# A two-layer attention and MLP kernel: spreading the reciprocal denominators by quarters of the TensorE array, residual loads one by one, and a different split of the first loads

## The chip, the core and the metric

The kernel runs on one core of a Trainium2 chip. The core has TensorE (PE, matmuls into PSUM, whose weight loads are listed as PEld), VectorE (DVE), ScalarE (ACT), GpSimd (POOL) and SyncE (SP, which here only issues DMAs); they run side by side and meet through semaphores. SBUF is the on-chip memory of 128 partitions, PSUM holds matmul results in eight banks of 128 x 512 f32. The metric is the device time of one execution in microseconds. Before the change the median of 3 runs is 766.76 us (766.41 to 767.0).

## What is computed

Four layers, A, B, A, B, on x of 2048 tokens x 576, the same weights each time. Both kinds normalise first (B twice) and add their result to x.

```python
def _A_ref(x, wqkv, wo):                      # linear attention, H = 32 heads of 18
    q, k, v = (x @ wqkv) split by three and by heads
    phi = lambda t: jnp.where(t > 0, t + 1, jnp.exp(t)) + 1e-6
    pq, pk = phi(q), phi(k)
    kv = jnp.einsum("bhsd,bhse->bhde", pk, v)
    z = jnp.einsum("bhsd->bhd", pk)
    num = jnp.einsum("bhqd,bhde->bhqe", pq, kv)
    den = jnp.einsum("bhqd,bhd->bhq", pq, z)[..., None] + 1e-6
    return merge_heads(num / den) @ wo
def _B_ref(x, w1, b1, w2, b2):                # MLP, F = 4608
    h = _gelu(_layernorm(x) @ w1 + b1)
    return h @ w2 + b2
x = x + _A_ref(_layernorm(x), ...); x = x + _B_ref(_layernorm(x), ...)   # and both once more
```

The division by `den` belongs to one head and one token. The kernel applies it to `pq`: each row of `pq` (a feature of a head) is multiplied by 1/den of its head.

## The kernel before

All weights lie in SBUF. The tokens are 16 tiles of 128 (`NT`) and 4 blocks of 512 (`c`, `NCA`), four tiles `j` to a block. The 576 features of q, k and v are in 5 groups of 7, 7, 7, 7 and 4 heads (`G`; 126 rows, the last 72). In this text the layers are counted 1 to 4; in the code `li` runs from 0, so the attention layers are `li == 0` (layer 1) and `li == 2` (layer 3, where `li > 0`).

The order of TensorE's instructions is the order in the source (`pe`, L138). The order on the other engines is made by a scheduler from the dependences, its own estimate of times and the order in the source; `tc.add_manual_dep(..., NOSYNC)` fixes that one instruction comes behind another on its engine without a semaphore. A tile from a pool waits until a buffer of its tag is free. PSUM is used as four single banks (`ps_h`, tag "h") and two pairs (`accA`, `accB`).

**The start.** `load_x0(t)` (L145) loads a token tile of x, `load_wqkv(part)` (L150) a third of the qkv weights in two DMAs (part 1 the keys, 2 the values). `chained` puts all of them on SP's queue in source order (L156 to L166). ACT's table for exp and ln is asked for at L176. Then, tile by tile, layer 1 normalises (`LNPipe`), transposes on TensorE, projects keys, values and part of the queries, and sums kv.

**The second half of an attention layer** (from L747). `kv_wo(g)` folds kv of a group with `wo`. Then, for a token block c:
- `den_stage(c)` (L750): 20 matmuls on 32-column quarters of the array sum the denominators; quarter j of the partitions has the 32 heads of token tile j. ACT takes ln and exp(-x), which gives `rden` [128 x 128] in bf16. `rden` has one buffer.
- `quad_stage(c)` (L769): DVE spreads `rden` to a [128 x 512] tile in which each token tile's columns have their own 32 rows and zeros elsewhere (`quad_mask`).
- `scale_stage(g, c)` (L779): one matmul of 512 columns by `head_bc` repeats each head's value over its 18 rows; ACT copies the product from PSUM to SBUF as bf16 (L788), and DVE multiplies `pq` by it (L789). With `direct` DVE reads PSUM and ACT does nothing.
- `wo_stage(t)` (L793): the output tile, ten matmuls into accA or accB in turn, then `residual` (L504): DVE adds x, SP stores the sum to `x_d`. For the first four tiles the normalisation of the next MLP layer is fed (L803) with a `hold` (ticks to wait), a `tp_at` (the output tile from which its transpose may run on TensorE) and the engine of its statistics: ACT for even tiles (two passes, L333 and L342, behind the inverted denominators), DVE for odd ones.

Block 0 goes first (L811 to L833), with the last deferred queries and the denominators of block 1. Then the loop over t (L834): in iteration t it prefetches the residual rows of tile t+4, runs `wo_stage(t)`, makes `quad_stage` of a block whose denominators have come, projects one group of queries if any is left (three in layer 1, one in layer 3), spreads groups 0 to 2 of the next block at j = 0 and groups 3 and 4 at j = 1, and at j = 1 sums the denominators of the block after that. At t = 13 ACT loads the table of gelu. One or two ticks of `LNPipe` follow.

**Residual rows.** In layer 1 they are loaded in pairs of tiles from x in bf16, in layer 3 one by one from `x_d` in f32 (`prefetch_xo`, L486) into a pool of 9 row buffers (tag "row"), which the sums also use. `turned` (L110) is the SBUF tile in which the MLP layers turn their normalised rows; in the attention loops it is idle.

The MLP layers (`LayerB`) run 36 groups of first-product matmuls on two halves of the array's rows, with gelu on ACT, and 16 tiles of second-product matmuls.

Of the kernel before, what the change touches and what calls it, by code (L numbers as in the profile page):

```python
# [8 lines left out]
ALU = mybir.AluOpType  # L9
# [6 lines left out]
P = 128  # L16
# [18 lines left out]
def build(tc, A_x, A_wqkv, A_wo, B_w1, B_b1, B_w2, B_b2, out, dbg=None, n_layers=4):  # L35
    nc = tc.nc
    dbg = dbg or {}
    with ExitStack() as ctx:
# [103 lines left out]
                pe_chain["last"] = inst.ins.name  # L142
            return inst

        def load_x0(t):  # L145
            x0 = blk.tile([P, D], BF16, name="x0", tag="blk")
            chained(nc.sync.dma_start(out=x0[:], in_=x_in[t * P:(t + 1) * P, :]))
            x0_tiles[t] = x0

        def load_wqkv(part):  # L150
# [2 lines left out]
                                      in_=A_wqkv[0:4 * P, cols].rearrange("(k p) n -> p k n", p=P)))  # L153
            chained(nc.sync.dma_start(out=wqkv_sb[0:64, 4, cols], in_=A_wqkv[4 * P:D, cols]))

        load_x0(0)  # L156
        load_x0(1)
        load_wqkv(1)
        load_x0(2)
        load_wqkv(2)  # L160
        load_x0(3)
        load_x0(4)
# [10 lines left out]
                pe(nc.tensor.matmul(warm_ps[:], lhsT=y_ring[NY - 1][:, 0:P], rhs=y_ring[NY - 1][:, 0:512],  # L173
                                    start=True, stop=True))

        nc.scalar.preload_act_table_set("natural_log_exp_and_others")  # L176
        nc.vector.memset(wqkv_sb[64:P, 4, :], 0.0)
        for vr in v_ring:
            nc.gpsimd.memset(vr[:, 4, 72:126], 0.0)
# [306 lines left out]
        def prefetch_xo(li, t, add_b2):  # L486
            if li == 0:
                if t % 2 == 0:
                    pair = rows.tile([P, 2, D], BF16, name="xo_pair", tag="row")
                    chained(nc.sync.dma_start(  # L490
                        out=pair[:], in_=x_in[t * P:(t + 2) * P, :].rearrange("(two p) d -> p two d", two=2)))
                    for i in range(2):
                        xo_of[(li, t + i)] = pair[:, i, :]
                return
            xo = row_tile("xo")
            load = nc.sync.dma_start(out=xo[:], in_=x_d[t])
            if not add_b2:
                behind(load, "landed")
            if add_b2:
                tc.add_manual_dep(load.ins, dve_last["sum"], NOSYNC, reason="no residual rows ahead of their stage")  # L500
                nc.gpsimd.tensor_tensor(out=xo[:], in0=xo[:], in1=b2_bc[:], op=ALU.add)  # L501
            xo_of[(li, t)] = xo[:]

        def residual(li, t, halves):  # L504
            xo = xo_of.pop((li, t))
            last = (li == n_layers - 1)
            if last:
                xn = rows.tile([P, 2 * D], BF16, name="xbf", tag="row")[:, 0:D]
            elif li == 0:
                xn = row_tile("xn")[:]  # L510
            else:
                xn = xo
            parts = [slice(h * HALF, (h + 1) * HALF) for h in range(2)] if last and t == NT - 1 else [slice(0, D)]
            for i, cols in enumerate(parts):
                if len(parts) == 2:
                    total = nc.vector.tensor_tensor(out=xn[:, cols], in0=halves[i][:, 0:HALF], in1=xo[:, cols], op=ALU.add)
                else:
                    total = nc.vector.tensor_tensor(out=xn[:, cols].rearrange("p (h n) -> p h n", h=2), in0=halves,  # L518
                                                    in1=xo[:, cols].rearrange("p (h n) -> p h n", h=2), op=ALU.add)
                dve_last["sum"] = total.ins.name  # L520
                if last:
                    nc.sync.dma_start(out=out_f[t * P:(t + 1) * P, cols], in_=xn[:, cols])
            if last:
                return None
            nc.sync.dma_start(out=x_d[t], in_=xn)
            return xn

        def layer_A(li, next_kind, pre_a1=None):
# [217 lines left out]

            quad_rden = {}  # L747
            rden_of = {}

            def den_stage(c, after=None, pair=None):  # L750
                if pair:
# [11 lines left out]
                if after is not None:  # L763
                    tc.add_manual_dep(log.ins, after, NOSYNC, reason="copies first")
                act_last["rden"] = nc.scalar.activation(out=rden[:], in_=dp[:, P:2 * P], func=ACT.Exp,
                                                        scale=-1.0).ins.name
                rden_of[c] = rden

            def quad_stage(c, after=None):  # L769
                quad = blk.tile([P, D], BF16, name="quad_rden", tag="blk")  # L770
# [8 lines left out]
            def scale_stage(g, c, pair=None, direct=False):  # L779
# [10 lines left out]
                                               in1=spread_rows[0:GR[g], 0:CA], op=ALU.mult)  # L790
                dve_last["mult"] = mult.ins.name

            def wo_stage(t):  # L793
                c, j = divmod(t, TPC)
                wp = ps_acc.tile([P, 2, 512], F32, name="wo_ps", tag=("accA", "accB")[t % 2])
# [4 lines left out]
                                              start=(g == 0), stop=(g == G - 1)))  # L800
                xn = residual(li, t, wp[:, :, 0:HALF])
                if xn is not None and next_kind == "B" and t < TPC:
                    lnp.feed(xn, t, "B", "pool", "act", hold=(2, 2, 6, 6)[t], tp_at=6 + 2 * t,  # L803
                             **(dict(after="sum") if t % 2 else dict(stats="act", after="rden")))

            for t in range(AHEAD):
                prefetch_xo(li, t, add_b2=False)
            if "b1" in bias_stage:
                bias_casts()
# [12 lines left out]
            if li == 0:  # L822
                late = [q_proj(*q_left.pop(0), defer=True)]
            for g in range(3):
                scale_stage(g, 0)
            kv_wo(4)
            scale_stage(3, 0, pair="accA")
            late.append(q_proj(*q_left.pop(0), defer=True))
# [4 lines left out]
                phi(after=act_last["rden"])  # L833
            for t in range(NT):  # L834
                c, j = divmod(t, TPC)
                if t + AHEAD < NT:
                    prefetch_xo(li, t + AHEAD, add_b2=False)
                wo_stage(t)
                for late in list(rden_of):
                    quad_stage(late, after=dve_last["sum"])  # L840
                if q_left:
                    q_proj(*q_left.pop(0))
                if c + 1 < NCA:
                    for g in ((0, 1, 2), (3, 4), (), ())[j]:
                        scale_stage(g, c + 1)
                if j == 1 and c + 2 < NCA:
                    den_stage(c + 2)
                if t == NT - 3:
                    warm_table(ACT.Gelu_apprx_tanh, act_last["copy"])
                state["wo"] = t  # L850
# [240 lines left out]
```

## Time and profile before

| | |
|---|---|
| median of 3 runs | 766.76 us |
| profiled execution, device time | 766.11 us |
| its span, first to last instruction | 764.4 us |
| key and query work of layer 1, up to its last kv sum | to about 69 us |
| layer 1: from there to the MLP's first matmul | 69 to 106 us |
| layer 2 (MLP) | 106 to 388 us |
| layer 3 (attention) | 388 to 479 us |
| layer 4 (MLP) | 479 to 764 us |

The profile shows one execution. The page has the busy time of each engine, the busy shares in 40 slices, the TensorE clock that was granted, the DMA queues, and the chain that ended last: followed back from the last instruction, at each step to what released it or to the instruction before it on its engine. In rows of the chain of waits the columns are start, length (both us from the span's start) and what ran. In rows of the timeline they are start, length, engine, line, operation, output<-input, shapes and count, with the idle time before it and what ended that in brackets. In rows of groups they are line, engine, operation, names, shapes, count, then busy us, mean ns of one, and idle time in front with its releasers. TensorE's records overlap: a matmul of 512 columns has a record of about 0.38 us, but the next one starts 0.22 us later.

### The profile page before, as it was taken

To read this page: it belongs to the slowest core of one execution; us is meant where nothing else is said; L and a number is where in the kernel's file an instruction comes from. 1 tells how busy PE (TensorE), PEld (TensorE's weight loads), DVE (VectorE), ACT (ScalarE), POOL (GpSimd) and SP (SyncE) were. 2 spreads that over 40 slices of the span, in tenths; PEclk is the share of its full clock that TensorE was granted. 3 is DMA by queue.
4 is the path that set the end of the run, shared out by engine and by line. 5 is a ranking of instruction groups with operands and counts; after the bars stand their busy time and mean duration, and the time that the engine had idled before them with its cause. 6 is when DMAs were issued, how large, how long until landed. Compare 5 with 4: busy or idle time off the path is not lost.

```text
span 764.4 us, 15650 instructions
## 1 busy us (share of the span) xinstructions
PE 758.8 (99%) x6522; PEld 492.1 (64%) x6522; DVE 271.6 (36%) x684; ACT 336.5 (44%) x751; POOL 123.4 (16%) x198
## 2 busy tenths in 40 slices
PE   8999999999999999999999999999999999999998
PEld 6776664675477457646777767447745764674476
DVE  7785963135113603400355678600240032000000
ACT  5888856304710650164056577570064036205600
POOL 4681222012000301200110004200020021001000
PEclk9999999999999999999999999999999999999999
DMA  9992473016401721330246007530231033011000
GB/s 262 270 299 49 158 275 85 17 47 178 110 24 63 203 62 42 97 85 1 75 120 215 1 16 245 206 81 17 62 105 41 16 125 81 9 32 55 2 9 24
DMA packets 80289, 73.82 MB, mean 97 GB/s; under 512 B 36698, under 2 KB 64858, under 8 KB 80218
## 3 DMA queue, kind: packets, MB, share of 16 engines
q1 hardware_dynamic: 80218, 72.82, 32.6%
q8 instruction: 51, 0.84, 0.5%
q14 instruction: 20, 0.16, 0.1%
HBM read 48.03 MB, written 24.77 MB: 95 GB/s over the span
## 4 chain that ended last, share of the span: by engine, by line
PE 98%; DVE 1%; DMA 1%; ACT 0%; SPq 0%; issue 0%
PE m_ps L972 36%; PE h_ps L914 20%; PE hp_ps L914 16%; PE q_ps L588 5%; PE wo_ps L798 5%; PE k_ps L540 3%; PE k_ps L612 3%; PE k_ps L629 2%; PE v_ps L561 1%; PE m_half L972 1%; PE v_ps L558 1%; PE rden_ps L784 1%; PE tp L423 1%; DMA wqkv_sb<-in_A_wqkv_dram 1%; PE kvacc L582 1%; PE k_tail L629 1%
## 5 line engine op out<-in xcount | busy, mean ns | idle before, releaser
L972 PE MATMUL m_ps<-w_sb,hT 128*128 128x288 bf16 x2232 | 274.8, 286 | 0.0
L972 PEld LDWEIGHTS <-hT 128*128 128x128 bf16 x2304 | 224.8, 98 | 59.8 <-issue 3.4
L914 PEld LDWEIGHTS <-w_sb 64*128 64x128 bf16 x2304 | 124.5, 94 | 136.5 <-issue 1.9
L914 PE MATMUL hp_ps<-yT,w_sb 64*128 64x512 bf16 x1152 | 178.0, 376 | 0.0
L914 PE MATMUL h_ps<-yT,w_sb 64*128 64x512 bf16 x1152 | 148.0, 376 | 0.0
L919 ACT COPY relay_sb<-relay_sb 128x1 f32<-128x1 f32 x144 | 28.6, 198 | 262.3 <-PE h_ps L914 220.0
L910 ACT ACTIVATE hT<-h_ps,b1T 128x512 bf16<-128x512 f32 x144 | 91.2, 684 | 44.4 <-PE h_ps L914 44.4
L374 POOL TENSOR_TENSOR ln_rstd<-ln_u,neg_half 128x1 f32<-128x1 f32 x64 | 36.6, 574 | 370.8 <-DVE ln_u L365 226.4
L910 ACT ACTIVATE hT<-hp_ps,b1T 128x512 bf16<-128x512 f32 x144 | 91.2, 693 | 0.0
L518 DVE TENSOR_TENSOR xbf<-m_ps,xo 128x576 bf16<-128x576 f32 x15 | 11.4, 757 | 212.9 <-PE m_ps L972 212.9
L518 DVE TENSOR_TENSOR xo<-m_ps,xo 128x576 f32<-128x576 f32 x16 | 12.1, 758 | 176.1 <-PE m_ps L972 176.1
L501 POOL TENSOR_TENSOR xo<-xo,b_bc 128x576 f32<-128x576 f32 x32 | 41.0, 1287 | 100.4 <-DMA xo<-x_d 63.7
L914 PE MATMUL h_ps<-yT,w_tail 64*128 64x512 bf16 x144 | 54.1, 376 | 0.0
L914 PE MATMUL hp_ps<-yT,w_tail 64*128 64x512 bf16 x144 | 54.1, 376 | 0.0
L588 PE MATMUL q_ps<-yT,wqkv_sb 128*126 128x512 bf16 (+1 forms) x200 | 49.8, 380 | 0.0
L798 PE MATMUL wo_ps<-kvwo,pq 126*128 126x288 bf16 (+1 forms) x320 | 43.3, 286 | 0.5 <-DVE pq L789 0.5
L914 PEld LDWEIGHTS <-w_tail 64*128 64x128 bf16 x288 | 27.1, 94 | 17.1
L798 PEld LDWEIGHTS <-pq 126*128 126x128 bf16 (+1 forms) x320 | 30.1, 97 | 10.5 <-DVE pq L789 1.0
L467 ACT ACTIVATE phi_e<-k_ps 128x288 bf16<-128x288 f32 x46 | 19.3, 419 | 38.8 <-PE k_ps L612 35.8
L588 PEld LDWEIGHTS <-wqkv_sb 128*126 128x126 bf16 (+1 forms) x200 | 24.9, 131 | 11.4 <-issue 0.2
L475 DVE TENSOR_SCALAR phi_e<-phi_e 128x288 bf16<-128x288 bf16 (+2 forms) x86 | 24.7, 288 | 20.1 <-ACT phi_e L467 19.4
L467 ACT ACTIVATE phi_e<-q_ps 126x512 bf16<-126x512 f32 (+1 forms) x40 | 23.8, 596 | 18.0 <-PE q_ps L588 18.0
(136 smaller groups left out, 657.0 us busy)
## 6 DMA issues: line engine op xcount, KB each, us to landing
xo<-x_d SPq DMA_DIRECT2D x48, 288.0 KB
x_d<-xo SPq DMA_DIRECT2D x32, 288.0 KB
xl<-x_d SPq DMA_DIRECT2D x24, 288.0 KB
y_d<-turned SPq DMA_DIRECT2D x40, 144.0 KB
w_sb<-in_B_w_dram SPq DMA_DIRECT2D x6, 864.0 KB
yT<-y_d SPq DMA_DIRECT2D x10, 512.0 KB
w_sb<-in_B_w_dram SPq DMA_DIRECT2D x9, 512.0 KB
x_d<-xn SPq DMA_DIRECT2D x16, 288.0 KB
```

What stands on the lines that cost most here:

```text
L374: nc.gpsimd.tensor_tensor(out=rstd[:], in0=it["u"][:], in1=neg_half[:], op=ALU.pow)
L467: exp = nc.scalar.activation(out=e_out, in_=ps_ap, func=ACT.Exp)
L475: low = nc.vector.tensor_scalar(out=e[0:rows, 0:n], in0=e[0:rows, 0:n], scalar1=1.0, scalar2=1e-6, op0=ALU.min, op1=ALU.add)
L501: nc.gpsimd.tensor_tensor(out=xo[:], in0=xo[:], in1=b2_bc[:], op=ALU.add)
L518: total = nc.vector.tensor_tensor(out=xn[:, cols].rearrange("p (h n) -> p h n", h=2), in0=halves, in1=xo[:, cols].rearrange("p (h n) -> p ...
L588: pe(nc.tensor.matmul(qp[0:GR[g], :], lhsT=wqkv_sb[:, k, GO[g]:GO[g] + GR[g]], rhs=yT[:, k, c * CA:(c + 1) * CA], start=(k == 0), stop=(k ...
L629: pe(nc.tensor.matmul(dst, lhsT=lhsT, rhs=pk, start=(t == 0), stop=(t == NT - 1)))
L798: pe(nc.tensor.matmul(wp[:, half, 0:HALF], lhsT=pq[(g, c)][0:GR[g], j * P:(j + 1) * P], rhs=kvwo[g][0:GR[g], half * HALF:(half + 1) * HALF ...
L910: act_last["gelu"] = nc.scalar.activation(out=to, in_=ps, func=ACT.Gelu_apprx_tanh, bias=b1T[:, f:f + 1], scale=1.0).ins.name
L914: mm = pe(nc.tensor.matmul(dst[n], lhsT=wt, rhs=mv, start=(seen[n] == 0), stop=(seen[n] == 8)))
L919: relay = nc.scalar.copy(out=relay_sb[:, 1:2], in_=relay_sb[:, 0:1])
L972: pe(nc.tensor.matmul(acc[half][:, 0:HALF], lhsT=hT[f][:, j * P:(j + 1) * P], rhs=w2_sb[:, f, half * HALF:(half + 1) * HALF], start=(f == ...
```

## The change

The four full groups of token blocks 1 to 3 are spread in a new way in both attention layers. `quarter_stage(c)` takes `rden` as it is: for each group and each token tile i one matmul of 32 rows (i's heads) and 128 columns, each i into a PSUM bank of its own, 16 matmuls in all. ACT then copies the four banks to `turned`. `quarter_scale(c, groups)` multiplies `pq` of these groups by it, behind the output tile's sum. Group 4 goes as before, so `quad_stage` stays. The steps move in the loop: for block 1 the quarter stage stands behind output tile 1, its multiplies, group 4 and the denominators of block 2 behind tile 2; the later blocks' quarter stages stand behind tiles 3 and 7, their multiplies behind the two tiles after those, the denominators of block 3 behind tile 5. The queries left stand behind tile 0 (one) and tile 2 (two).

In layer 1 group 0 of block 0 is multiplied out of PSUM. In layer 3 six residual tiles are prefetched in place of four ahead of the loop, then one in each iteration from 1 to 10, and the loads of tiles 9 and up stand behind the last store. The statistics of the fed tiles change engines (DVE for even tiles, ACT for odd ones), with other holds, and in layer 1 other transposes. At the start ACT's table is asked for first, and token tiles 1 and 2 are loaded from ACT's queue behind it.

```diff
-        def load_x0(t):
+        def load_x0(t, by_act=False):
             x0 = blk.tile([P, D], BF16, name="x0", tag="blk")
-            chained(nc.sync.dma_start(out=x0[:], in_=x_in[t * P:(t + 1) * P, :]))
+            if by_act:
+                load = nc.scalar.dma_start(out=x0[:], in_=x_in[t * P:(t + 1) * P, :])
+                tc.add_manual_dep(load.ins, table.ins.name, NOSYNC, reason="table first")
+            else:
+                chained(nc.sync.dma_start(out=x0[:], in_=x_in[t * P:(t + 1) * P, :]))
...
+        table = nc.scalar.preload_act_table_set("natural_log_exp_and_others")
         load_x0(0)
-        load_x0(1)
+        load_x0(1, by_act=True)
         load_wqkv(1)
-        load_x0(2)
+        load_x0(2, by_act=True)
         load_wqkv(2)
...
-        nc.scalar.preload_act_table_set("natural_log_exp_and_others")
...
                 behind(load, "landed")
+                if t >= 9:
+                    tc.add_manual_dep(load.ins, sp_last["store"], NOSYNC, reason="stores first")
...
-            nc.sync.dma_start(out=x_d[t], in_=xn)
+            sp_last["store"] = nc.sync.dma_start(out=x_d[t], in_=xn).ins.name
...
+                rden_now["tile"] = rden
...
+            def quarter_stage(c):
+
+                rden = rden_now["tile"]
+                banks = [ps_h.tile([P, 512], F32, name="rden_ps", tag="h") for _ in range(4)]
+                for g in range(4):
+                    for i in range(4):
+                        rows = slice(32 * i, 32 * (i + 1))
+                        pe(nc.tensor.matmul(banks[i][0:126, g * P:(g + 1) * P], lhsT=head_bc[rows, g, 0:126],
+                                            rhs=rden[rows, :], start=True, stop=True))
+                spread_rows = turned[:].rearrange("p a t c -> p (a t c)").rearrange("p (i w) -> p i w", i=4)
+                for i in range(4):
+                    act_last["copy"] = nc.scalar.copy(out=spread_rows[0:126, i, 0:4 * P], in_=banks[i][0:126, :]).ins.name
+
+            def quarter_scale(c, groups, after):
+                spread_rows = turned[:].rearrange("p a t c -> p (a t c)").rearrange("p (i w) -> p i w", i=4)
+                for g in groups:
+                    scaled = pq[(g, c)][0:126, 0:CA].rearrange("p (i n) -> p i n", i=4)
+                    mult = nc.vector.tensor_tensor(out=scaled, in0=scaled,
+                                                   in1=spread_rows[0:126, :, g * P:(g + 1) * P], op=ALU.mult)
+                    tc.add_manual_dep(mult.ins, after, NOSYNC, reason="sums first")
+                    dve_last["mult"] = mult.ins.name
...
-                    lnp.feed(xn, t, "B", "pool", "act", hold=(2, 2, 6, 6)[t], tp_at=6 + 2 * t,
-                             **(dict(after="sum") if t % 2 else dict(stats="act", after="rden")))
-
-            for t in range(AHEAD):
+                    lnp.feed(xn, t, "B", "pool", "act", hold=(2, 2, 2, 4)[t] if li > 0 else (2, 8, 8, 10)[t], tp_at=6 + 2 * t if li > 0 else (6, 10, 11, 14)[t],
+                             **(dict(after="sum") if t % 2 == 0 else dict(stats="act", after="rden")))
+
+            for t in range(AHEAD if li == 0 else AHEAD + 2):
                 prefetch_xo(li, t, add_b2=False)
...
             for g in range(3):
-                scale_stage(g, 0)
+                scale_stage(g, 0, direct=(li == 0 and g == 0))
...
-                if t + AHEAD < NT:
-                    prefetch_xo(li, t + AHEAD, add_b2=False)
+                if li == 0 and t + AHEAD < NT or 0 < t < NT - AHEAD - 1 and li > 0:
+                    prefetch_xo(li, t + AHEAD + (li > 0), add_b2=False)
                 wo_stage(t)
-                for late in list(rden_of):
-                    quad_stage(late, after=dve_last["sum"])
-                if q_left:
+                total = dve_last["sum"]
+                if c + 1 < NCA:
+                    for g in ((), (), (0, 1, 2, 3), ())[j] if c == 0 else ((0, 1), (2, 3), (), ())[j]:
+                        quarter_scale(c + 1, (g,), after=total)
+                    if t == 1:
+                        quarter_stage(1)
+                    if j == 3 and c + 2 < NCA:
+                        quarter_stage(c + 2)
+                    if j == (2 if c == 0 else 0):
+                        scale_stage(4, c + 1)
+                if j == (2 if c == 0 else 1) and c + 2 < NCA:
+                    den_stage(c + 2)
+                    if c > 0:
+                        quad_stage(c + 2, after=total)
+                if t == 3:
+                    quad_stage(2, after=total)
+                if q_left and t in (0, 2):
                     q_proj(*q_left.pop(0))
-                if c + 1 < NCA:
-                    for g in ((0, 1, 2), (3, 4), (), ())[j]:
-                        scale_stage(g, c + 1)
-                if j == 1 and c + 2 < NCA:
-                    den_stage(c + 2)
+                    if t == 2:
+                        q_proj(*q_left.pop(0))
```

1 line of the change is left out of this document (added).

## Prediction

> **What bounds the kernel now.** I read the page's busy shares first, then its chain, then the chain in order of time around the two places that change.
>
> ```profile
> span 764.4 us, 15650 instructions
> PE 758.8 (99%) x6522; PEld 492.1 (64%) x6522; DVE 271.6 (36%) x684; ACT 336.5 (44%) x751; POOL 123.4 (16%) x198
> PEclk9999999999999999999999999999999999999999
> PE 98%; DVE 1%; DMA 1%; ACT 0%; SPq 0%; issue 0%
> ```
>
> TensorE is busy 99% of the span at the full granted clock, and 98% of the chain that ended last is its own. So time is gained only by fewer TensorE columns, or in the few places where TensorE stands. The changed loop of layer 1, and the place just in front of it, in the chain of waits (start, length, what):
>
> ```profile
> 74.22 0.54 ACT kvwo L745
> 74.76 0.49 ACT rden_bc L788
> 75.25 0.02 issue
> 75.28 0.42 DVE pq L789
> 75.70 0.66 DVE kvwo L743
> 76.36 1.61 DVE pq L789 x4
> 77.98 0.05 issue
> 78.02 0.91 PE wo_ps L798 x6
> 78.94 1.08 PE q_ps L588 x5
> 80.02 0.65 PE rden_ps L784 x3
> 80.66 1.23 PE wo_ps L798 x10
> 81.90 1.08 PE q_ps L588 x5
> 82.98 0.43 PE rden_ps L784 x2
> 83.41 0.40 PE den_ps L758 x20
> 83.81 1.34 PE wo_ps L798 x10
> 92.74 0.28 PE tp L423 x5
> ```
>
> Two things are to be seen. From 78.02 on every piece is PE: an output tile costs 1.23 us, a spread matmul 0.65/3 = 0.217 us, and nothing waits. From 74.22 to 78.02 it is ACT and then DVE that set the time. The third place is the start, in the same view and then in the timeline:
>
> ```profile
> 0.80 0.39 SPq L147
> 1.24 0.42 SPq L147
> 1.71 5.17 DMA wqkv_sb<-in_A_wqkv_dram
> 6.92 0.77 PE k_ps L540 x5
> ```
>
> ```profile
> 0.79 1.28 ACT L176 ACT_TABLE_LOAD   x1 [0.79 <-PEq L1075]
> 3.01 0.46 DVE L351 BATCH_NORM_STATS2 ln_st<-x 128x6 f32<-128x288 bf16 x1
> 4.18 0.45 DVE L351 BATCH_NORM_STATS2 ln_st<-x 128x6 f32<-128x288 bf16 x1
> 4.93 0.43 DVE L395 TENSOR_SCALAR y_ring<-x,ln_mv,ln_rstd 128x576 bf16<-128x576 bf16 x1
> 6.33 0.10 PEld L540 LDWEIGHTS <-yT 128*128 128x128 bf16 x1 [0.52 <-ACT yT L426]
> ```
>
> The first keys start at 6.92, when the key weights have landed; their other operand was there at 6.33.
>
> **The spread by quarters** (token blocks 1 to 3 of layers 1 and 3, so six times). Removed: four full matmuls of 512 columns, 4 x 0.217 = 0.87 us. The fifth, of group 4, stays. Added: 16 matmuls of 32 rows and 128 columns, each quarter of the array with its own rows and its own PSUM bank. No row shows such a quarter. The nearest is the denominator stage: 20 matmuls of 128 columns, four side by side on column quarters, in 0.40 us, and the ten matmuls behind it take 1.34 in place of 1.23, so 0.51 with the change of shape. That is five waves of about 0.056 us (tp: five full weight loads with 128 columns in 0.28) and 0.23 for entering and leaving. Four waves give 0.45; I add 0.03 because the weights are 126 columns wide, not 32: 0.48. Gain 0.87 - 0.48 = 0.39, six times 2.3 us. From both sides: perfect waves and only the 0.11 behind them, 0.22 + 0.11 = 0.33, gain 0.54 each (3.2); sixteen weight loads one behind the other at the rate of tp, 16 x 0.056 + 0.11 = 1.0, loss 0.13 each (-0.8). I stay near the denominator stage, since it too is four independent parts of the array.
>
> The Trainium skill, "TensorE: Matmul & The Clock Gate", section "Part 3: Packing small matmuls", gives 3.07 times for four row tiles of 32 rows with 512 columns. By it the quarter stage would take 0.87/3.07 = 0.28 us and the six would bring 3.5 us; no run here shows it yet, and the denominator stage is slower than that per wave, so I don't go by it.
>
> The four copies out of PSUM and four multiplies stay as many and as large; they are only moved to another iteration, and the multiplies read a strided tile. A multiply of a group now needs all four copies rather than one.
>
> **What the moved steps must fit under.** The quarter stage wants all four small banks at once, with the denominators of the stage before. Between two quarter stages of layer 3's first block TensorE runs an output tile, the group-4 spread, the denominators and an output tile: 1.23 + 0.22 + 0.51 + 1.23 = 3.19 us. ACT has five copies and the two passes that invert the denominators in that time:
>
> ```profile
> L765 ACT ACTIVATE rden<-den_ps 128x128 bf16<-128x128 f32 x6 | 1.7, 278 | 0.2
> L762 ACT ACTIVATE den_ps<-den_ps 128x128 f32<-128x128 f32 x6 | 1.7, 275 | 1.4 <-PE den_ps L758 1.4
> ```
>
> 5 x 0.49 + 0.55 + some 0.3 for the hand-overs = 3.3, so about 0.2 us of wait once. In layer 1 the two moved query projections (2 x 1.08) stand there too, and their two passes on ACT (about 1.0 behind the second one) end some 0.2 behind the next output tile: 0.2 again. Behind the waiting quarter stage stands the whole TensorE queue. On DVE the four multiplies and the fifth (about 4 x 0.36 + 0.42, from x4 in 1.61 with the long direct one in it) follow the fourth copy, with a sum in front; in layer 3 they end about when the next block's output needs group 4: 0.2. In the later blocks three more output tiles (3.7 us) lie between, and this cover hides all. Together -0.6 us, between 0 and the second rival's price.
>
> **The direct multiply of layer 1.** Group 0 of block 0 is no longer copied by ACT.
>
> ```profile
> 74.06 0.81 PE L784 MATMUL rden_ps<-quad_rden,head_bc 128*128 128x512 bf16 x3
> 77.29 0.68 DVE L789 TENSOR_TENSOR pq<-pq,rden_ps 72x512 bf16<-72x512 bf16 x1
> ```
>
> Its product is in PSUM at about 74.5 (74.06 and 0.38, which is the 0.81 of three overlapping matmuls less two steps of 0.217), and a multiply out of PSUM takes 0.68 instead of 0.42. DVE starts at 74.5 instead of 75.28 and has 0.26 more to do: the chain ends about 0.5 earlier. ACT's copies for groups 1 to 3 (0.49 each, from 74.76 on) are late next and hold it to 0.3-0.4. I take 0.35, bounds 0 and 0.5.
>
> **The start.** The second and third token tiles go out on ACT's queue behind its table load. On SP the key weights move up by one issue, 0.47 us (1.24 to 1.71), and the value weights by two. The gain is at most 6.92 - 6.33 = 0.59, where the first tile itself is late next. On the other side, the second tile's statistics (4.18) stand on DVE ahead of the first tile's normalisation (4.93). If ACT issues only when the table is there, 0.79 + 1.28 = 2.07, the tile takes the 2.21 us of the first one (0.80 to 3.01) and lands at 4.3, and up to 0.7 later where it shares the engines with the weights (576 KB in 5.17 us less 2.2). At 5.0 the first keys would start at 7.17, 0.25 late. I take +0.2, bounds -0.25 and +0.59.
>
> **Residual loads, statistics, transposes: nothing.** Layer 3's late loads queue on SP behind the store of the output tile before; behind a waiting load stand the next stores and loads, and the sums five tiles (6 us) on wait for them.
>
> ```profile
> 480.00 0.76 DVE L518 TENSOR_TENSOR xo<-wo_ps,xo 128x576 f32<-128x576 f32 x1 [1.00 <-DMA xo<-x_d]
> 480.25 1.24 PE L914 MATMUL hp_ps<-yT,w_sb 64*128 64x512 bf16 x8
> 102.38 0.69 ACT L430 COPY yT<-tp 128x640 bf16<-128x640 bf16 x1 [1.32 <-PE tp L423]
> ```
>
> Even a residual that is 1.00 us late today holds only DVE; TensorE goes on at 480.25 in the other accumulator. Layer 1's last transpose moves behind the fifteenth output tile: its copy (0.69, with 0.2 of hand-over) must fit under the sixteenth (1.23). It does, by 0.3; were the copy queued behind a table load of 1.28, it would cost about 1 us once.
>
> **Sum**: 2.3 + 0.35 + 0.2 - 0.6 = 2.25 us less. The profiled execution took 766.11 with its span of 764.4 and would take 763.86; it lies 0.65 under the median of the runs shown, 766.76, so the median becomes 764.5.
>
> **Rivals.** (1) The weight loads of the four quarters go one behind the other, so the change doesn't do what it says: -0.8 + 0.35 + 0.2 - 0.6 = 0.85 slower, 767.6. For: a 126-column weight load is as long as a 128-column stream (tp). Against: the denominators' 20 loads fit in 0.40. (2) Slower: ACT's queue takes the normalisation's statistics ahead of the quarter's copies.
>
> ```profile
> 85.42 0.68 ACT L333 ACTIVATE ln_dump<-xn 128x576 bf16<-128x576 f32 x1
> 86.22 0.78 ACT L342 ACTIVATE ln_dump<-xn,ln_mv 128x576 bf16<-128x576 f32 x1
> ```
>
> Such a pair holds ACT 1.6 us (85.42 to 87.00). The next spread needs a bank 1.23 us behind the quarter stage; it would come after 0.16 (a matmul's record, 0.38, less its step), 1.6 and a copy of 0.49, a wait of 1.0. In the first block of each layer the multiplies come later with the copies, and the next block's output waits the other 0.6. It decides from the point where a pair stands right ahead of the copies. Four pairs and two such blocks: 4 x 1.0 + 2 x 0.6 = 5.2 lost against 2.85 gained, 2.35 slower, 769.1. For: today the pairs follow the inverted denominators directly, and the quarter stages wait for those too. Against: the new holds put the pairs elsewhere. (3) Everything overlaps: 3.2 + 0.5 + 0.5, no waits, 762.6. (4) The ACT loads go out another table load's length late: the second tile lands 1.3 us behind 5.0 and the first keys at 8.4, 1.5 late; 2.05 - 1.5 = 0.55 faster, 766.2. Against it:
>
> ```profile
> 98.99 1.28 ACT L448 ACT_TABLE_LOAD   x1
> 100.28 0.20 ACT L448 ACTIVATE act_dummy<-neg_half 128x1 f32<-128x1 f32 x1
> ```
>
> ACT's next instruction starts 0.01 us behind the load. The Trainium skill, "ScalarE: Activation LUTs", section "What ACT_TABLE_LOAD costs", adds a drain of about 1.38 us to each load, which would be this rival; these rows don't show it.
>
> **Chances and range.** Forecast 0.55, serial loads 0.14, ACT's order 0.17, full overlap 0.09, late table 0.05. What a measurement of this kernel tells from no change is about 0.2%, 1.5 us. The forecast's own range is 763.2 to 766.0. Serial loads and the late table lie above it; ACT's order with one or two pairs gives 766.5 to 768, with all four more. I reach to 762.3 and 768.2, which leaves out half of ACT's order and a part of the full overlap. Faster: three quarters of the forecast (0.42; its upper end is within what a measurement tells) and full overlap, 0.51 together. Slower: ACT's order and the worst of the serial loads, 0.20. The rest, 0.29, is the same.
>
> **What would show it.** The 16 quarter matmuls in some 0.45 us of the chain, six times, with the next output tile near 1.34; near 1.0 is rival 1. A wait on PE for `rden_bc` copies or `pq` behind the first quarter stages sizes the -0.6; pairs L333/L342 ahead of copies are rival 2. The first keys below 6.92, and the DVE chain in front of layer 1's output ending 0.35 earlier than today relative to them. The MLP stages must not change; if they do, or if the multiplies on the strided tile take much over 0.42, the prediction is wrong for a reason not in it.

## The result and the profile after

The median after the change is 764.57 us (22 runs), beside 766.41 us for the kernel before on the same chips (22 runs): ratio 0.9981, 95% interval 0.9974 to 0.9987, so 1.84 us faster. The profiled executions differ by 1.60 us: 766.11 before (span 764.4), 764.51 after (span 762.8). Of the 22 runs, 17 lie between 764.45 and 764.75 and five at 765.86 to 766.66; the kernel before shows no such group, and the experiments come back to it.

The page after, the lines that answer to the first ones of the prediction:

```profile
span 762.8 us, 15788 instructions
PE 757.0 (99%) x6594; PEld 491.0 (64%) x6594; DVE 271.5 (36%) x684; ACT 336.1 (44%) x750; POOL 125.3 (16%) x198
PE 97%; DVE 2%; DMA 0%; issue 0%; ACT 0%; ACTq 0%
```

TensorE lost 1.8 us of work (758.8 to 757.0) although it has 72 matmuls more, and the span fell by 1.6. DVE has gone from 1% to 2% of the chain: a part of the gain has turned into waits for DVE.

The chain of waits in layer 1 after the change (start, length, what):

```profile
69.09 0.26 PE kvacc L588 x5
...
78.77 1.08 PE q_ps L594 x5
...
81.08 0.38 PE rden_ps L808 x16
81.46 1.34 PE wo_ps L828 x10
...
104.77 1.18 PE h_ps L955 x9
```

The quarter stage takes 0.38 us, and the output tile behind it 1.34 in place of 1.23: 0.49 together, where four full matmuls took 0.87. The first output tile ends at 78.77, before at 78.94, although the last kv sum starts 0.29 later (69.09) than in the kernel before. That one, and the other landmarks of before, in its chain:

```profile
68.80 0.26 PE kvacc L582 x5
106.05 1.18 PE h_ps L914 x9
445.56 0.30 PE z_ps L693 x5
479.44 1.18 PE h_ps L914 x9
```

From the end of the first output tile to the MLP's first matmul layer 1 took 106.05 - 78.94 = 27.11 us and takes 104.77 - 78.77 = 26.00 now: 1.11 less, of three stages' 3 x 0.38 = 1.14. So nothing waits there. In layer 3 it is otherwise. The same chain of after:

```profile
444.29 0.30 PE z_ps L699 x5
...
460.71 0.33 DVE quad_rden L779
...
464.33 0.68 DVE xo L524
465.05 1.39 PE wo_ps L828 x10
477.85 1.18 PE h_ps L955 x9
```

From `z_ps` to the MLP it was 479.44 - 445.56 = 33.88 and is 477.85 - 444.29 = 33.56: only 0.32 of the 1.14 arrived. The lost 0.82 lies where DVE stands in the chain. The timeline there:

```profile
456.46 0.45 DVE L355 BATCH_NORM_STATS2 ln_st<-xo 128x6 f32<-128x288 f32 x1
459.13 0.45 PE L808 MATMUL rden_ps<-rden,head_bc 32*126 32x128 bf16 x16
459.62 0.78 ACT L346 ACTIVATE ln_dump<-xo,ln_mv 128x576 bf16<-128x576 f32 x1
460.40 2.03 ACT L812 CAST turned<-rden_ps 126x512 bf16<-126x512 f32 x4
460.97 0.45 DVE L355 BATCH_NORM_STATS2 ln_st<-xo 128x6 f32<-128x288 f32 x1
461.10 0.10 PEld L792 LDWEIGHTS <-head_bc 128*128 128x128 bf16 x1 [0.39 <-DVE quad_rden L779]
```

DVE takes the statistics of two tiles in layer 3 as it did before, but then they started at 460.66 and 467.18. The timeline of the kernel before:

```profile
460.66 0.45 DVE L351 BATCH_NORM_STATS2 ln_st<-xo 128x6 f32<-128x288 f32 x1
467.18 0.45 DVE L351 BATCH_NORM_STATS2 ln_st<-xo 128x6 f32<-128x288 f32 x1
```

Now they are those of tiles 0 and 2 and start at 456.46 and 460.97 (about 1.25 us each with their other steps), both in the stretch in which the first two quarter stages' multiplies come due. DVE is behind there: at 461.10 TensorE waits for the masked tile of group 4, and at 465.05 for a sum that frees the accumulator. The second quarter stage's product is ready by 459.6, but a pair of statistics on ACT goes first (the second pass at 459.62), and the copies begin at 460.40. A third thing stands in this stretch:

```profile
462.53 0.83 POOL L395 TENSOR_SCALAR y_ring<-xo,ln_rstd,ln_nmr 128x576 bf16<-128x576 f32 x1
462.81 1.19 DVE L818 TENSOR_TENSOR pq<-pq,turned 126x512 bf16<-126x512 bf16 x2
```

The first of these two multiplies took 0.81 us, the longest of the 24 (median 0.42), while POOL normalised a tile beside it. Its extra 0.39 lies on the chain in front of the wait at 465.05.

The start, from the chain and the timeline of after:

```profile
0.80 2.84 DMA x<-in_A_x_dram
6.98 0.79 PE k_ps L546 x5
14.29 0.45 PE tp L427 x5
```

```profile
0.79 1.28 ACT L160 ACT_TABLE_LOAD   x1 [0.79 <-PEq L1116]
0.82 0.87 ACTq L148 DMA_DIRECT2D x<-in_A_x_dram  x2
3.66 0.46 DVE L355 BATCH_NORM_STATS2 ln_st<-x 128x6 f32<-128x288 bf16 x1 [0.72 <-DMA x<-in_A_x_dram]
```

ACT issued both loads at 0.82, while its table was loading. But the first tile's statistics start at 3.66 in place of 3.01. The chain that ends in the first keys is now the first tile's transfer, no longer that of the key weights. The first keys start 0.06 later than before, and the fourth tile's transposes (14.29) wait for its normalisation, which costs 0.21 more: 0.29 with the rest. DVE took that tile's statistics at 11.52 in place of 11.12, behind a multiply that lasted 0.77 (0.30 before) while POOL normalised the third tile.

### The profile page after: what moved, and what is told of

It is laid out like the page before. It is cut to its first block, busy times and chain, and to the rows that moved or that the text cites. A ratio compares the mean times of both kernels' runs of the same rounds, so it can differ in the third digit from the quotient of the medians.

```text
span 762.8 us, 15788 instructions
## 1 busy us (share of the span) xinstructions
PE 757.0 (99%) x6594; PEld 491.0 (64%) x6594; DVE 271.5 (36%) x684; ACT 336.1 (44%) x750; POOL 125.3 (16%) x198
## 4 chain that ended last, share of the span: by engine, by line
PE 97%; DVE 2%; DMA 0%; issue 0%; ACT 0%; ACTq 0%
PE m_ps L1013 36%; PE h_ps L955 20%; PE hp_ps L955 16%; PE q_ps L594 6%; PE wo_ps L828 4%; PE k_ps L546 3%; PE k_ps L618 3%; PE k_ps L635 2%; PE v_ps L567 1%; PE m_half L1013 1%; PE v_ps L564 1%; PE tp L427 1%; PE kvacc L588 1%; PE k_tail L635 1%; DVE xo L524 0%; DMA x<-in_A_x_dram 0%
```

## The experiments

**Is the gain TensorE's columns?** The quarter stage is replaced by four full matmuls of 512 columns, with every move of the change kept; block 2's masked tile is made one output tile earlier.

```diff
-                    for i in range(4):
-                        pe(nc.tensor.matmul(banks[i][0:126, g * P:(g + 1) * P], lhsT=head_bc[rows, g, 0:126],
-                                            rhs=rden[rows, :], start=True, stop=True))
+                    pe(nc.tensor.matmul(banks[g][:, 0:CA], lhsT=head_bc[:, g, :], rhs=quad_rden[c][:, 0:CA],
+                                        start=True, stop=True))
...
```

> The changed kernel with all its moves, but each quarter stage made of four full-array matmuls of 512 columns on the masked tile, four banks and four copies as before; the denominators' spread for block 2 on DVE moves one tile earlier for it. Theory: TensorE's columns are what the change gains, 0.38 us six times, so this is 2.3 us slower than the changed kernel, 766.9, and the stage takes 0.87 in place of 0.49 with its change of shape. Rival: the moves make the gain and the time stays within 0.5 us of 764.6.

Measured 767.15 us, ratio to the kernel before 1.0014 (1.0005 to 1.0023). Its chain in layer 1:

```profile
81.03 0.86 PE rden_ps L805 x4
```

It is 2.58 us above the changed kernel. Six times 0.38 are 2.28, and its layer 3 has one wait of 1.07 us in place of the 0.82: 0.25, together 2.53. Without the quarters the rest of the change, the new start included, is 0.76 us slower than the kernel before (766.39 beside it).

**What does one quarter matmul cost?** Each of the 16 is done twice, with the same result.

```diff
-                for g in range(4):
+                for g in (0, 1, 2, 3, 0, 1, 2, 3):
```

> After with each of the 16 quarter matmuls of a stage done twice (the same values written again), everything else as it is. Theory: the quarter matmuls of the four row groups run beside each other, so a further sixteen cost what sixteen starts take, some 13 ns each, 0.21 us per stage and 6 x 0.21 = 1.3 us in all: 765.9. Rival 1: a further group costs its whole 0.38 us, 2.3 in all: 766.85. Rival 2: no overlap between row groups, 16 x 0.055 = 0.88 per stage, 5.3 in all: 769.8.

```profile
80.98 0.61 PE rden_ps L808 x32
```

Sixteen more cost 0.61 - 0.38 = 0.23 us, 14 ns each: as much as four waves of 0.056 (a 128-column matmul in the rows of `tp`, 0.28 for five). So four run beside each other. If the first sixteen cost the same 0.23, the other 0.15 of the 0.38, with the 0.11 behind it, is the price of entering and leaving. The time, 765.42 (ratio 0.9991, 0.9982 to 1.0), rose by 0.85 and not by the expected 1.3: up to the MLP of layer 1 it rose by 0.59 (three stages' 0.69, less 0.11 because the last kv sum came earlier), in layer 3's loop by 0.22 only, where the longer stage fills waits for DVE that are there anyway.

**Does the order of the row quarters matter?** The four groups of one row quarter are issued one after the other, then the next quarter's.

```diff
-                for g in range(4):
-                    for i in range(4):
+                for i in range(4):
+                    for g in range(4):
```

> The changed kernel with the 16 quarter matmuls in another order: all four groups of one row quarter, then the next quarter, so that neighbours share rows and bank. Theory: the 0.38 us of a stage come from four row quarters working side by side, so in turn a stage takes 0.8 to 1.0 us (16 times 0.05 to 0.06) and the kernel is 2.5 to 3.5 us slower than the changed one, about 767.6. Rival: TensorE finds the overlap whatever the order, the stage stays near 0.4 and the time at 764.6.

```profile
82.98 0.41 PE rden_ps L808 x16
```

The theory was wrong: 0.41 in place of 0.38, and a median of 764.67 us (0.9983, 0.9974 to 0.9992). TensorE overlaps the quarters also when four matmuls of the same rows stand in sequence. Its profiled execution took 766.54, one of two such in ten, and shows one way to such a time. First its chain, then its windows of 2 us (length, then for PE, PEld, DVE, ACT and POOL the busy time, then granted clock, DMA share, GB/s):

```profile
1.23 6.32 DMA wqkv_sb<-in_A_wqkv_dram
7.59 1.31 PE k_ps L546 x5
```

```profile
8.00:10.00 2.00, 2.00 (x13) 1.44 (x12) 0.53 (x4) 1.07 (x3) 0.00 (x0) 0.50 0.81 206
10.00:12.00 2.00, 2.00 (x14) 1.39 (x13) 0.30 (x2) 0.89 (x4) 1.65 (x3) 0.73 1.07 350
```

The first tile was early this time (statistics at 3.33), but the key weights landed only at 7.55. TensorE had stood 0.86 us in front of the first transposes and 0.97 in front of the first keys, and then the granted clock fell to 0.50 (8 to 10 us) and was at 0.73 over the next two. Five keys took 1.31 in place of 0.79, and the last kv sum came at 70.99, 1.9 behind that of after. The five high runs of the changed kernel don't have this fall of the clock: its mean on record is 0.998 for this execution and 1.0 for each of the five. The kernel with the old residual loads, further down, has the changed kernel's start, and its profiled execution shows a second way:

```profile
6.08 0.71 PE L427 MATMUL tp<-ident,y_ring 128*128 128x128 bf16 x5 [0.75 <-DVE y_ring L399]
7.44 1.40 PE L544 MATMUL k_ps<-wqkv_sb,yT 128*128 128x288 bf16 x5
```

The changed kernel stood as long in front of its first transposes (0.73), but they took 0.45 and the keys 0.79. Here the clock is listed as 1.00 all the while, and the last kv sum came at 70.51, 1.42 behind that of after. By size and clock this fits the five; a trace of one of them was not taken.

**The start undone, and the start alone.** In the first kernel the changed kernel keeps the start of before; in the second the kernel before gets the new start and nothing else.

```diff
-        table = nc.scalar.preload_act_table_set("natural_log_exp_and_others")
...
-        load_x0(1, by_act=True)
+        load_x0(1)
...
-        load_x0(2, by_act=True)
+        load_x0(2)
...
+        nc.scalar.preload_act_table_set("natural_log_exp_and_others")
```

> The changed kernel with the start as before: the token tiles 1 and 2 go out on SP again and the table is asked for where it was. Theory: sharing the DMA engines between two queues made the first token tile land 0.65 us later and cost 0.29 us by the end of layer 1's sums, so this is 0.3 us faster than the changed kernel, 764.3, and the spread of its runs above 765.8 goes too if it comes from the first loads. Rival: the delay is absorbed before the MLP, 764.6, and the spread stays.

> The kernel before with nothing but the new start. Theory: 0.1 to 0.4 us slower than before, the first statistics near 3.66 instead of 3.01, and some runs 1.4 to 2 us longer if the spread comes from the first loads. Rival (the prediction's term): 0.2 us faster, first keys below 6.92.

Start undone: 764.29 us (nine runs, 764.07 to 764.63; ratio 0.9975, 0.9965 to 0.9984). Start alone: 766.47 beside 766.39 (ratio 1.0005, 0.9997 to 1.0014), three of eleven runs at 767.76 to 767.89. By the medians the new start loses 0.28 us beside the other changes; alone it loses 0.08, which is within the noise. The high runs come with it: they are 22 of the 99 runs of the eight kernels that load from ACT's queue (the one with the old residual loads left out), and none of 28 in the three that have the start of before with other changes. The kernel before had 2 in 129 (768.23 and 768.48), both with a mean clock of 0.998.

**Which part of the start?** First only the second tile goes out on ACT's queue. Then none does, but the key weights keep their early place on SP.

```diff
         load_x0(1, by_act=True)
         load_wqkv(1)
-        load_x0(2, by_act=True)
+        load_x0(2)
```

> After with the third token tile loaded from SP's queue as before; the second one stays on ACT's queue. Theory: the first tile is late because the two tiles from ACT share the DMA engines with it; with one of them gone its statistics start about half as late, near 3.3 us in place of 3.66 (before 3.01), and the time is 764.4 to 764.5. Rival: the first tile is late because the key weights are issued 0.47 us earlier behind it; then it stays at 3.66 and the first keys at 7.0. Whether the runs 1 to 2 us above the rest, which 5 of 22 runs of after show, come from the two loads or from one: with one they become rarer if it is the sharing with the key weights.

```diff
         load_x0(0)
-        load_x0(1, by_act=True)
         load_wqkv(1)
-        load_x0(2, by_act=True)
+        load_x0(1)
+        load_x0(2)
```

> After with tiles 1 and 2 back on SP's queue, but behind the two key loads, which so keep the early place that after gives them (second and third issue on SP). With one tile left on ACT's queue the first statistics stayed at 3.68 us. Theory A: a load on ACT's queue, however much it carries, holds the first tile up; without any it is back at 3.0 us, and no run lies 1 to 2 us above the rest. Theory B: the key weights issued 0.47 us earlier hold it up; it stays near 3.6, and such runs stay. By A the first keys wait for the key weights (6.4 to 7.0 us) or for the second tile's statistics, whose tile comes 1.1 us later: 764.1 to 764.9.

The timelines, one tile on ACT's queue and then none:

```profile
3.68 0.46 DVE L355 BATCH_NORM_STATS2 ln_st<-x 128x6 f32<-128x288 bf16 x1 [0.74 <-DMA x<-in_A_x_dram]
```

```profile
3.06 0.46 DVE L355 BATCH_NORM_STATS2 ln_st<-x 128x6 f32<-128x288 bf16 x1
6.38 0.46 DVE L355 BATCH_NORM_STATS2 ln_st<-x 128x6 f32<-128x288 bf16 x1 [2.06 <-DMA x<-in_A_x_dram]
```

With one tile the first is as late as with two (3.68), against my theory that half the bytes cost half; the median is 764.55 (0.9979, 0.9971 to 0.9988), four of twelve runs at 765.87 to 766.13. With none on ACT's queue the first tile is back at 3.06 although the key weights are issued early. So one load beside it on ACT's queue holds the first tile up by 0.65, and the early place of the key weights does not. The size varies: in the nine profiled executions with such a load the first statistics start at 3.33 to 3.76, in the five without at 3.01 to 3.06. Whether it is the queue, or only that this load goes out 0.02 us behind the first one (0.80 and 0.82), no run separates. But behind the key weights the second tile comes at 6.38, the first keys wait until 8.50, and the time is 767.05 (1.0011, 1.0002 to 1.002) where I had expected 764.1 to 764.9: how long a 144 KB tile takes behind 576 KB of weights I had put far too low. These runs lie between 765.78 and 768.34 without a group of their own, so whether the high runs vanish with the loads on ACT's queue they don't tell.

**Is layer 3's loss its holds?** Layer 3 gets layer 1's holds and transposes.

```diff
-  hold=(2, 2, 2, 4)[t] if li > 0 else (2, 8, 8, 10)[t], tp_at=6 + 2 * t if li > 0 else (6, 10, 11, 14)[t],
+  hold=(2, 8, 8, 10)[t], tp_at=(6, 10, 11, 14)[t],
```

> The changed kernel with layer 1's holds and transpose times in layer 3 too. Theory: TensorE's 0.82 us of waits in layer 3 come from a DVE backlog in which tiles 0 and 2 have 1.25 us of statistics each, and from a pair of ACT passes in front of the second quarter copies; with tiles 1 to 3 held back the waits of 0.25 and 0.47 us go and the kernel is 0.5 to 0.7 us faster than the changed one, 764.0. Rival: the sums and multiplies alone fill DVE, the waits stay within 0.2 us and the time is 764.5.

764.16 us (0.9978, 0.9969 to 0.9987), 0.41 less. The loop from `z_ps` (444.16) to the MLP (477.25) takes 33.09 in place of 33.56: the wait of 0.47 for the sum is gone, that for the masked tile remains. Three of its runs lie at 765.57 to 766.03. The edit moves three things at once: the second statistics on DVE (to 465.11), the pair on ACT (the copies now begin at 459.67) and POOL's normalisation (no multiply takes over 0.43). Which of them made the wait, it doesn't separate.

**The rest of the wait.** To take that too, this kernel has the start of before, layer 1's holds, and the group-4 spreads of blocks 2 and 3 one output tile later.

```diff
-                    if j == (2 if c == 0 else 0):
+                    if j == (2 if c == 0 else 1):
```

> The changed kernel with the start as before, layer 1's holds in layer 3, and group 4 of blocks 2 and 3 spread one output tile later, so that it no longer waits for the masked tile on DVE. Theory: the three parts add, 0.28 + 0.42 + 0.25 us faster than the changed kernel, 763.6, with no wait over 0.1 us left in layer 3's loop and no runs above 765. Rival: with group 4 later another wait takes its place (its multiply in front of the next block's output tiles), 763.9.

766.2 us (0.9997, 0.9989 to 1.0006), where I had expected 763.6; without the later group 4 the same kernel takes 764.17 (the last experiment). Its timeline in layer 1:

```profile
93.58 0.78 ACT L346 ACTIVATE ln_dump<-xn,ln_mv 128x576 bf16<-128x576 f32 x1
94.36 2.02 ACT L812 CAST turned<-rden_ps 126x512 bf16<-126x512 f32 x4
96.41 1.15 DVE L818 TENSOR_TENSOR pq<-pq,turned 126x512 bf16<-126x512 bf16 x2 [1.28 <-ACT turned L812]
97.48 0.75 DVE L524 TENSOR_TENSOR xn<-wo_ps,xo_pair 128x576 f32<-128x576 f32 x1
98.28 1.39 PE L828 MATMUL wo_ps<-kvwo,pq 126*128 126x288 bf16 x10 [0.98 <-DVE xn L524]
```

The scheduler put a pair of ACT statistics ahead of the copies; DVE's multiplies wait 1.28 for them; the sum stands behind the multiplies; and TensorE stands 0.98 us for the sum's accumulator. The wait came in both layers (98.28 and 471.92). The first link is that of the prediction's second rival, a pair of passes ahead of the copies. The last link differs: TensorE waits not for a bank that the copies hold, but for an accumulator behind late multiplies. An edit that moved something else called it up.

**The direct multiply undone.**

```diff
-                scale_stage(g, 0, direct=(li == 0 and g == 0))
+                scale_stage(g, 0)
```

> The changed kernel with group 0 of block 0 in layer 1 copied by ACT as before. Theory: the direct multiply brought 0.46 us (the first output tile ends that much earlier against the start of the stretch), so this is 0.4 to 0.5 us slower than the changed kernel, 765.0. Rival: a part of it is given back later in the loop, at most 0.2 us slower, 764.7.

764.94 us (0.9985, 0.9976 to 0.9994): 0.37 more, with a wait of 0.44 back in front of layer 1's first output tile.

**Layer 3's residual loads as before**, beside all else of the change.

```diff
-                if t >= 9:
-                    tc.add_manual_dep(load.ins, sp_last["store"], NOSYNC, reason="stores first")
...
-            for t in range(AHEAD if li == 0 else AHEAD + 2):
+            for t in range(AHEAD):
...
-                if li == 0 and t + AHEAD < NT or 0 < t < NT - AHEAD - 1 and li > 0:
-                    prefetch_xo(li, t + AHEAD + (li > 0), add_b2=False)
+                if t + AHEAD < NT:
+                    prefetch_xo(li, t + AHEAD, add_b2=False)
```

> The changed kernel with layer 3's residual loads as before: four ahead, tile t+4 in iteration t, no order behind the stores. Theory: these loads hide nothing and cost nothing on TensorE, 764.4 to 764.8, with DVE waiting for a late residual near the end of layer 3 again. Rival: the order keeps a store or a load off DVE's full stretch, and without it TensorE's waits in layer 3 grow from 0.82 us by 0.5 or more, 765.1.

772.49 us (1.0082, 1.007 to 1.0095): 7.9 us above the changed kernel, where I had expected none. Its chain, its PE waits (us in total, times, longest), and its windows:

```profile
475.19 6.16 DMA xo<-x_d
...
482.28 2.56 PE wo_ps L826 x10
```

```profile
PE wo_ps L826 <- DVE xo L522: 4.4, 3, 2.9
```

```profile
482.00:484.00 2.00, 1.72 (x8) 1.07 (x8) 0.93 (x2) 0.00 (x0) 0.00 (x0) 0.50 1.05 407
484.00:486.00 2.00, 2.00 (x10) 0.65 (x10) 0.76 (x1) 0.00 (x0) 0.00 (x0) 0.50 1.04 387
```

The last tiles' residuals arrive late; the sums wait, and TensorE with them: 4.4 us, of which 0.3 is the wait for a sum that the changed kernel has too. Then the granted clock is 0.50 to 0.53 from 482 to 488 us, and the last output tile takes 2.56 in place of 1.23. Of the 8.50 us by which this profiled execution (773.01) is longer, 1.41 are lost at its start, as shown above, 5.58 in layer 3's loop (39.14 in place of 33.56) and 1.5 in the MLP's first matmuls. Why the loads are late only beside the other moves (the kernel before had them in this order, and its DVE waited 1.00 once) I did not separate: a load that waits for one of the nine row buffers would hold SP's queue with the stores behind it, and the stores free the buffers, but no run changed the one without the other.

**The two gains together**: the start of before and layer 1's holds in layer 3.

> After with the start as before (tiles 1 and 2 and the table issued as before) and layer 3's holds and due times as in layer 1. Theory: the two edits act in different places (the first 10 us; the waits in layer 3's loop) and their gains add up: 764.57 - 0.28 (start) - 0.41 (holds) = 763.9, with no runs 1 to 2 us above the rest, if those come from the start alone. Rival: the runs with the holds of layer 1 are dearer for another reason than the start, and a quarter of the runs still lies at 765.5 or above; or the two gains overlap, and the time stays at 764.2.

764.17 us median (eight runs, 763.22 to 764.51; ratio 0.997, 0.9959 to 0.9981), against the kernel before the best of all, but by its median not apart from the two kernels with one of the edits each (764.29 and 764.16). So the median is the 764.2 of the rival, not the 763.9 of the theory; but no run lies 1 to 2 us above the rest, as the theory had it. Its profiled execution (763.44) shows both gains, in the chain, so that the rival's overlap is not seen there:

```profile
1.71 4.75 DMA wqkv_sb<-in_A_wqkv_dram
68.38 0.26 PE kvacc L588 x5
443.58 0.30 PE z_ps L699 x5
476.67 1.18 PE h_ps L955 x9
```

The last kv sum comes 0.71 before that of after (69.09), 0.42 of it because the key weights landed at 6.46 in this execution and at 6.88 in that of the kernel before; and layer 3's loop takes 476.67 - 443.58 = 33.09, as with the holds alone. Whether the weights' landing also makes the spread of its runs wasn't traced.

## Why the prediction was right, and where it was not

**The time** came out as forecast, 764.57 for 764.5, but that it is so close is luck: two errors met. I had forecast 2.25 less. The profiles show 1.60, and the medians 1.84; and the median of three that I started from, 766.76, lay 0.35 above that of 22. What was right is the main term.

**The quarters**, 2.3, were right: six times 0.38 are 2.28, and a stage costs 0.49 where I had 0.48. The choice to stay near the denominator stage carried this, and the doubled matmuls bear out its parts, four waves and a fixed price for entering and leaving. Neither bound came near: not the serial weight loads (1.0, first rival) and not the perfect overlap (0.33, third rival). The Trainium skill, "TensorE: Matmul & The Clock Gate", section "Part 3: Packing small matmuls", gives 3.07 times for four row tiles with 512 columns; my estimate from it was 0.28 us per stage. The trace doesn't bear that out for a stage this short: by the measurement the stage as a whole gains 0.87/0.49 = 1.8 times; the doubled half alone, 0.87/0.23 = 3.8 times. The price of entering and leaving makes the difference.

**The direct multiply**, 0.35, was right in its mechanism and a little small: from the last kv sum to the end of the first output tile it was 78.94 - 68.80 = 10.14 and is 78.77 - 69.09 = 9.68, a gain of 0.46; undoing it costs 0.37. ACT's copies of groups 1 to 3, which I had late next, did not take it back.

**The start**, +0.2, was wrong, in sign too: -0.29 by the last kv sum, beyond its lower bound of -0.25. The step that failed is "the first tile itself is late next", where I took that tile's landing at 3.0 as given and looked for the loss in the second tile alone. The loads did go out in time, and the fourth rival (a late table) did not come. What they do is hold up the first tile, by 0.65, for which none of my bounds had a row. At the first keys 0.06 of it is left; most of the 0.29 is the fourth tile's normalisation, which I hadn't followed. The Trainium skill, "DMA: Bandwidth & Descriptors", section "Issuing engines are not separate DMA queues", has the sentence I should have weighed: loads from several engines run on the same 16 DMA engines, and only the issue time is saved. The trace agrees and shows the price.

**The waits**, -0.6, came to -0.85, in other places. Layer 1's 0.2 didn't come: 0.03. Layer 3's were 0.82 for 0.4. (ACT's half of that 0.4 was high by its own sum, too: 3.3 less 3.19 is 0.11, not about 0.2.) The step that failed is the one that costs the statistics at "nothing". I counted what DVE has to do behind the fourth copy without them; but as the new holds place them, both tiles' statistics, 2.5 us of DVE, fall into the stretch of the first two quarter stages. With layer 1's holds 0.47 of the wait is gone. That the holds cost it is shown; how much of it is the statistics on DVE, how much the pair on ACT and how much the multiply of 0.81 beside POOL is not. Such a multiply (0.80 to 0.81) is in each of the eight traces that have the quarters and the new holds in layer 3, and in neither of the two that change only the holds, or the holds and the start.

**Rival 2** was in the changed kernel once (the copies at 460.40), inside these 0.82, and not at four places; the group-4 experiment shows that a pair ahead of the copies can cost about 1 us a time, though by way of the accumulator, not of a bank.

**Residual loads: nothing** holds for the changed kernel: no sum waits for them any more. But as a reason it was wrong. That TensorE goes on in the other accumulator is true of one late tile; with two in a row it stood 4.1 us, and the clock fell with it. The new order of these loads is not an extra but what the other moves need.

The terms as measured: 2.28 + 0.46 - 0.29 - 0.85 = 1.60, the difference of the two spans. The MLP stages didn't change, and the strided multiplies take what the plain ones took (1.42 for four).

## What to carry to other kernels

Packing small matmuls on quarters of the array costs something once per stage and little per matmul: here, by the doubled stage, about 0.26 us and 14 ns each (126 columns of weights, 128 of data). Put as many as possible into one stage. An engine that is 36% busy on average can be full in the one stretch where moved work comes due: look there. An earlier issue on a second queue can delay the transfer that everything waits for, so cost the first one, not the one moved.

## What was not expected of the hardware

After a short stand TensorE can run at a lower rate for some microseconds, which costs more than the stand itself. With stands of 0.86 and 0.97 us the granted clock was 0.50 over two microseconds and 0.73 over the next two. With one stand of 0.75 us five keys took 1.40 in place of 0.79, though the clock is listed as 1.00; the changed kernel, with a stand of 0.73, shows nothing of it. With the second tile behind the key weights TensorE stood 2.2 us in front of the first transposes, and they too ran at their usual 0.45. So the length of a stand doesn't decide; what does is open.

The order in which quarter matmuls are issued hardly matters (0.38 and 0.41 us for 16): row quarters overlap also when four of the same rows stand in front.

A single 144 KB load on ACT's queue delays the first tile on SP's queue as much as two do (3.68 and 3.66 us, 3.06 without).

A DVE multiply can take twice its time while POOL normalises a tile: 0.81 in place of 0.42 in layer 3, 0.77 in place of 0.30 at the start. That POOL is the cause is not shown by a run of its own.
